# A gated mix of linear attention and a state-space convolution: masked kv left in PSUM, VectorE's work reordered in the passage between the two halves, two q products moved, and tiles placed at multiples of 256 bytes

## The chip, the cores and the metric

The kernel runs on one core of one Trainium2 chip. The metric is device time in microseconds (us), the median of the runs shown. Five engines appear: PE (TensorE; PEld is its weight load), DVE (VectorE), ACT (ScalarE), POOL (GpSimd) and SP (SyncE, which issues all DMAs).

## The reference

`x` has 2048 rows of 448. The result is a gated sum of two branches over the same `x`:

```python
g = _sigmoid((x * gate_w).sum(-1, keepdims=True))
a = _A_ref(x, A_wqkv, A_wo)              # linear attention, 16 heads of 28
b = _B_ref(x, ...) # causal convolution with a generated kernel K, plus u * D_skip
return g * a + (1 - g) * b

# in _A_ref, with phi(t) = where(t > 0, t + 1, exp(t)) + 1e-6
kv = jnp.einsum("bhsd,bhse->bhde", pk, v)
z = jnp.einsum("bhsd->bhd", pk)
num = jnp.einsum("bhqd,bhde->bhqe", pq, kv)
den = jnp.einsum("bhqd,bhd->bhq", pq, z)[..., None] + 1e-6
o = num / den                             # then @ wo
```

`kv` and `z` are sums over all 2048 rows, so no row's attention can be finished before every row's k has been read.

## The kernel before

The 2048 rows are 16 blocks of 128, numbered `c` = 0 to 15. Everything is float32; a large operand is split into a high and a low part (`split_t`, `split_n`, `k_high`, `k_low` and so on), and a product is made of high by high, low by high and high by low.

**First half.** For each block PE makes the k product of block `c + 1` (11 matmuls, tile `k` or `v1`), one or two products with a triangular matrix (tile `v`, for the convolution), the q product of block `c` (11 matmuls, tile `q`), and `do_g(c)`, which adds the block's 11 matmuls of phi(k) against x into four PSUM banks `g0` to `g3`, open over all blocks. ACT and DVE apply phi, POOL makes low parts and the skip term.

**Passage.** Block 15 is the last to go into `g`. Then, written out by hand:
`gs` is the copy of `g0..g3` to SBUF (four ACT copies). `inter` makes `z`, the carry of the convolution, and returns `carry`, one DVE instruction on the part of it that goes to `rc`. `kv_products(r)` multiplies `gs` by `wv`: for `r` = 1 heads' groups 2 and 3 into PSUM bank `k`, for `r` = 0 groups 0 and 1 into `tr`. `kv_split` multiplies the result by a block-diagonal mask (DVE, from PSUM into the SBUF tile `kv`), `kv_high` rounds it to `kvh` (ACT), `kv_low` makes `kvl`, the rest (DVE). `m_products(j)` multiplies group `j` by `wo` (three matmuls, tile `m`); `m_high` (ACT) and `m_low` (DVE) split that into the two halves of `wk2` (named `wk` in the profile) for `j` = 0 to 2 and into `shl` for `j` = 3. Four small DMAs then carry rows of `shl` into `wk2`.

**Normalization.** Per block: `norm_a(c)` is POOL's product `prod` of phi(q) by z; `norm_b(c)` is DVE's sum of it by heads (tile `den`, L530); `norm_d` is three small DVE instructions on it (L534, reciprocal L536, copy L539), below called a *den set* together with the DVE part of `norm_c`; `norm_c(c)` is one small DVE and two POOL products that give `pn`. `norm_bd` is `norm_b` and `norm_d`.

**Second half.** For each block, `turn(c)`: four PE transposes of `pn` into bank `tr`, split into `th` by ACT (high, L594) and DVE (low, L595); `tail(c)`, an ACT copy; `attend(c)`, 11 matmuls of `th` against `wk2` and `rc` (tile `a`); `final_b`, the DVE instruction that adds the two branches (tile `ot`), and its store. Loop step `c` prepares `turn(c + 1)`, `norm_c(c + 2)` and the later blocks' sums.

Within an engine instructions run in the order in which the program issues them. PSUM has eight banks: `q`, `k`, `v0`, `v1` for the whole kernel, and four that hold `g0..g3` first and two `tr` and two `a` afterwards. SBUF tiles come from pools laid out one behind the other: `const` first, then `xp`, `xt`, `xn` and `tp`. `QW` is the row pitch of the split weights `wqh` and `wql`, in float32 elements.

Of the kernel before, what the change touches and what calls it, by code (L numbers as in the profile page):

```python
# [15 lines left out]
P = 128  # L16
S = 2048
D = 448
H = 16
# [3 lines left out]
J = 4  # L23
DJ = D // J
# [5 lines left out]
PARTS = ((("x", 0), ("w", 1)), (("w", 2), ("w", 3)), (("w", 0), ("x", 1)))  # L30
FIRST = 2 * NAT + J * D
QA = 1
QW = D + 16
VS = {c: (2 * c - 10, 2 * c - 9) for c in range(5, 11)} | {c: (c + 1,) for c in range(11, NC - 1)}
SMALL = 2.0 ** -70
FLAT = 2.0 ** 35
# [1 line left out]
DS = 12  # L38
DT = 4 * (DH - DS)
# [94 lines left out]
def gated_mix_kernel(ctx: ExitStack, tc: tile.TileContext, xin, wq_d, wvo_d, abc_d, ldt_d, dsk_d,  # L134
                     turn_d, cst_d, first_d, gin_d, lag_d, out):
    nc = tc.nc
    PE, ACT, DVE, POOL, SP = nc.tensor, nc.scalar, nc.vector, nc.gpsimd, nc.sync
# [23 lines left out]
    mask, gcat, sel = cst[:DJ, :DJ], cst[:UZ, DJ:DJ + RX], cst[:, DJ + RX:]  # L161
# [15 lines left out]
    tp = work.enter_context(tc.tile_pool(name="tp", bufs=2))  # L177
# [21 lines left out]
    o = 0  # L199
    for part in PARTS:  # L200
# [8 lines left out]
        o = e  # L209
# [17 lines left out]
    def low(eng, o, r, h):  # L227
        eng.tensor_tensor(out=o, in0=r, in1=h.bitcast(F32), op=ALU.subtract)  # L228
# [78 lines left out]
    def pieces(c, wh, wl, n, tag, last=None):  # L307
        o = ps.tile([P, 512], F32, name=tag, tag=tag)
        h, l = ([xt[c][:, i + k * P:i + (k + 1) * P] for k in range(J)] for i in (0, NAT))
        hh, lh, hl = ([(a[k], w[:, k]) for k in range(J)] for a, w in ((h, wh), (l, wh), (h, wl)))  # L310
        hl = hl[1:]
        if last == "x":
            seq = hh + hl + lh
        else:
            seq = [p for k in range(J) for p in (hh[k], lh[k])] + hl
            if last == "w":
                seq = seq[2:6] + seq[8:9] + seq[6:8] + seq[9:] + seq[:2]

        def run(count):
            for _ in range(min(count, len(seq))):  # L320
                a, b = seq.pop(0)
                run.n += 1
                PE.matmul(o[:, :n], lhsT=a, rhs=b, start=run.n == 1, stop=not seq)  # L323
        run.n = 0
        return o, run
# [93 lines left out]
    w = xt[0] = xt_p.tile([P, 2 * NAT], F32R, name="xt", tag="t")  # L419
# [32 lines left out]
    qo = project(0, wqh, wql, D + 2, "q", "w")  # L452
# [3 lines left out]
    qo = project(1, wqh, wql, D + 2, "v0")  # L456
# [5 lines left out]
    for c in range(2, NC - 2):  # L462
# [17 lines left out]
        qo = project(c, wqh, wql, D + 2, "q")  # L480
# [29 lines left out]
        for j in {11: (0, 1), 12: (2, 3)}.get(c, ()):  # L510
            w = xn_p.tile([P, NX], F32R, name="wo", tag="n")[:DJ, :2 * D].rearrange("p (i d) -> p i d", i=2)
# [9 lines left out]
    pn, th, tl, pd, dn, dp = {}, {}, {}, {}, {}, []  # L521

    def norm_a(c):
        pd[c] = tp.tile([P, D], F32, name="prod", tag="pk")
        POOL.tensor_tensor(out=pd[c], in0=pq[:, c], in1=zb, op=ALU.mult)  # L525

    def norm_b(c):
        if not dp:
            dp.append(ps.tile([P, 512], F32, name="den", tag="v1")[:, :NC * H].rearrange("p (c h) -> p c h", c=NC))
        DVE.tensor_reduce(out=dp[0][:, c], in_=pd.pop(c).rearrange("p (h d) -> p h d", h=H), op=ALU.add, axis=AX.X)  # L530

    def norm_d(c, n, copy=DVE.tensor_copy):
        r = dp[0][:, c:c + n]
        DVE.scalar_tensor_tensor(out=r, in0=r, scalar=1e-6, in1=e1[:, c:c + n, None].to_broadcast([P, n, H]),  # L534
                                 op0=ALU.add, op1=ALU.mult)
# [3 lines left out]
        copy(dn[c // 2][:, c % 2:c % 2 + n], r)  # L539

    def norm_bd(c):
        norm_b(c)
        norm_d(c, 1)
# [24 lines left out]
    def gates_a(a, b):  # L568
        return og[:, a:b]
# [20 lines left out]
    def turn_split(c, o):  # L590
        t = xt_p.tile([P, 2, J, P], F32R, name="th", tag="t")
        h, l = th[c], tl[c] = t[:, 0], t[:, 1]
        ov = o.rearrange("p (j t) -> p j t", j=J)
        ACT.copy(h, ov)  # L594
        DVE.tensor_tensor(out=l, in0=ov, in1=h.bitcast(F32), op=ALU.subtract)  # L595
# [29 lines left out]
    c = NC - 2  # L625
# [7 lines left out]
    low(POOL, uw[UL:], u[UL:], uw[UL:])  # L633
    k_high(c + 1)
    k_low(c + 1)
    zh, zl = (tp.tile([P, D], F32R, name=n, tag=t) for n, t in (("zh", "w"), ("zl", "pk")))
    qo = project(c, wqh, wql, D + 2, "q")
    do_g(c, (0, 1, 2))
    zo = ps.tile([P, 512], F32, name="zo", tag="v0")
# [15 lines left out]
    for i in range(4):  # L655
        do_g(c + 1, (i,))
        ACT.copy(gs[i], g[i][:, :D])
        if i == 2:
            gates_b(gates_a(1, NC - 1), g[0])
    gates_c(NC - 2, g[0], "pkl")()  # L660
    norm_b(1)
    qo, q_run = pieces(c + 1, wqh, wql, D + 2, "q")
    for i in range(5):
        phi(i)
    gps.close()
# [41 lines left out]
        return kvp  # L707

    def kv_split(r, kvp):
        m = 3 if r else 2  # L710
        DVE.tensor_tensor(out=kv[:, 2 * r:m],
                          in0=kvp[:DJ, 2 * r * DJ:m * DJ].rearrange("p (j d) -> p j d", d=DJ),
                          in1=mask[:, None, :].to_broadcast([DJ, m - 2 * r, DJ]), op=ALU.mult)
        if r:
            a, b = (w.rearrange("p (h d) -> p h d", h=4) for w in (kvp[:DJ, 3 * DJ:4 * DJ], mask))
            DVE.tensor_tensor(out=kv[:, 3, :DT].rearrange("p (h d) -> p h d", h=4), in0=a[:, :, DS:], in1=b[:, :, DS:],
                              op=ALU.mult)
            a, b = (w[:, :, :DS].rearrange("p h (j d) -> p h j d", j=3) for w in (a, b))
            DVE.tensor_tensor(out=kv[:, 3, DT:].rearrange("p (j h d) -> p h j d", j=3, h=4), in0=a, in1=b, op=ALU.mult)

    def kv_high(r):
        rs = slice(2 * r, 2 * r + 2)
        ACT.copy(kvh[:, rs], kv[:, rs])

    def kv_low(r):
        rs = slice(2 * r, 2 * r + 2)
# [12 lines left out]
    o3 = m_products(3, ps, "k")  # L739
    o2 = m_products(2, ps, "v0")  # L740
    m_high(3, o3)
    kv_high(0)
    m_low(3, o3)
    kv_low(0)
    m_high(2, o2)
    for j in (2, 0, 1):
        SP.dma_start(out=wk2[DJ:, :, j].bitcast(F32), in_=shl[DT + 16 * j:DT + 16 * j + 16].bitcast(F32))
# [166 lines left out]
```

## Time and profile before

| | |
|---|---|
| median of 3 runs | 179.42 us (178.81, 179.42, 181.05) |
| the profiled execution | 178.89 us, of which the span from its first to its last instruction is 177.1 us |
| granted PE clock | 1.0 in all slices |
| DMA | 18.61 MB, mean 105 GB/s |

A profile row of the timeline gives the start in us from the span's start, the duration in us, the engine, the line, the operation, output <- inputs, shapes, the count, and in brackets how long the engine had been idle before and who ended the wait. Starts of neighbouring rows may overlap, since an engine begins an instruction before the one ahead has fully ended. In the chain of waits a row is start, duration and what the end of the run was waiting for at that time.

### The profile page before, as it was taken

How to read it: one execution, taken by the hardware profiler on the slowest of the kernel's cores; microseconds unless marked ns; L12 is line 12 of the kernel's file. 1: busy time of each engine (PE TensorE's matmuls, PEld its weight loads, DVE VectorE, ACT ScalarE, POOL GpSimd, SP SyncE). 2: the span in 40 equal slices, each digit the busy share in tenths (PEclk: the TensorE clock that was granted, in tenths of full speed). 3: DMA queues.
4: the chain of work that ended last, by engine and by line, in shares of the span. 5: the costliest groups of instructions: out<-in, count | busy, mean ns of one | idle time of the engine just before them, and what ended most of it. 6: DMA issues, size and time to landing. Idle time of an engine off the chain costs nothing.

```text
span 177.1 us, 2803 instructions
## 1 busy us (share of the span) xinstructions
PE 170.5 (96%) x876; PEld 151.6 (86%) x876; DVE 113.4 (64%) x244; ACT 96.2 (54%) x220; POOL 121.1 (68%) x128
## 2 busy tenths in 40 slices
PE   6999999999999999999999999999889999999991
PEld 2699999999999999999989999988678999999991
DVE  1747538698857274462824619376999988977451
ACT  3789388874536244272435753464645555564541
POOL 5167476977349969688599999439089999893100
PEclk9999999999999999999999999999999999999999
DMA  5999973095003303032133000000121212222313
GB/s 174 414 316 269 249 223 127 8 418 227 4 1 120 106 16 119 5 120 75 45 121 123 0 0 1 0 2 5 21 47 52 105 74 86 104 75 82 111 55 104
DMA packets 7963, 18.61 MB, mean 105 GB/s; under 512 B 2045, under 2 KB 4810, under 8 KB 7818
## 3 DMA queue, kind: packets, MB, share of 16 engines
q1 hardware_dynamic: 7946, 18.41, 31.6%
q8 instruction: 7, 0.11, 0.3%
q14 instruction: 10, 0.08, 0.2%
HBM read 14.38 MB, written 3.67 MB: 102 GB/s over the span
## 4 chain that ended last, share of the span: by engine, by line
PE 91%; DVE 4%; DMA 2%; ACT 1%; issue 0%; DVEq 0%; ACTq 0%
PE a L612 21%; PE g L392 20%; PE q L323 18%; PE k L323 16%; PE v L323 6%; PE tr L587 3%; DMA y<-in 2%; PE v L400 2%; PE v L399 2%; PE k L706 1%; DVE kvl L228 1%; DVE wk L694 1%; PE m L686 0%; DVE rc L677 0%; PE q L250 0%; DVE den L530 0%
## 5 line engine op out<-in xcount | busy, mean ns | idle before, releaser
L612 PE MATMUL a<-wk,th 128*128 128x448 f32 (+1 forms) x170 | 36.9, 363 | 0.7 <-DVE wk L694 0.7
L392 PE MATMUL g<-pkh,xn 128*128 128x448 f32 x112 | 35.6, 366 | 0.0
L612 PEld LDWEIGHTS a<-wk,th 128*128 128x128 f32 x170 | 29.5, 189 | 2.9 <-DVE wk L694 0.9
L323 PE MATMUL k<-wk,xt 128*128 128x448 f32 x132 | 29.6, 368 | 0.2 <-ACT wk L421 0.2
L351 DVE SCALAR_TENSOR_TENSOR k<-k,e 128x448 f32<-128x448 f32 x12 | 7.6, 632 | 32.1 <-ACT e L350 32.1
L323 PE MATMUL q<-wqh,xt 128*128 128x450 f32 x120 | 28.0, 370 | 0.0
L323 PEld LDWEIGHTS k<-wk,xt 128*128 128x128 f32 x132 | 24.6, 188 | 3.1 <-ACT wk L421 0.7
L412 POOL TENSOR_TENSOR y<-y,t 128x448 f32<-128x448 f32 x16 | 18.8, 1175 | 12.3 <-DVE t L404 11.9
L228 POOL TENSOR_TENSOR xn<-xr,xn 128x448 fp32r<-128x448 f32 x16 | 19.3, 1203 | 9.2 <-ACT xn L238 9.0
L323 PEld LDWEIGHTS q<-wqh,xt 128*128 128x128 f32 x120 | 22.5, 189 | 2.2 <-issue 0.2
L392 PE MATMUL g<-pkl,xn 128*128 128x448 f32 x64 | 23.4, 366 | 0.0
L392 PEld LDWEIGHTS g<-pkh,xn 128*128 128x128 f32 x112 | 21.0, 188 | 2.5
L349 ACT ACTIVATE e<-k 128x448 f32<-128x448 f32 x12 | 6.5, 546 | 28.0 <-PE k L323 27.9
L525 POOL TENSOR_TENSOR prod<-pq,zb 128x448 f32<-128x448 f32 x16 | 18.4, 1159 | 4.3 <-ACT zb L647 3.1
L244 POOL TENSOR_TENSOR y<-xr,rows 128x448 f32<-128x448 f32 x16 | 18.9, 1184 | 0.0
L228 POOL TENSOR_TENSOR xt<-xr,xt 128x512 fp32r<-128x512 f32 x14 | 18.2, 1299 | 0.4 <-ACT xt L232 0.4
L550 POOL TENSOR_TENSOR pn<-pq,den 128x336 f32<-128x336 f32 x16 | 12.1, 754 | 8.3 <-DVE den L539 4.4
L617 DVE SCALAR_TENSOR_TENSOR ot<-y,og,a 128x448 f32<-128x448 f32 (+1 forms) x17 | 10.6, 626 | 5.6 <-PE a L612 5.5
L595 DVE TENSOR_TENSOR th<-tr,th 128x512 fp32r<-128x512 f32 x16 | 11.0, 690 | 3.0 <-ACT th L594 2.5
L594 ACT CAST th<-tr 128x512 fp32r<-128x512 f32 x16 | 9.4, 590 | 5.5 <-PE tr L587 5.3
L392 PEld LDWEIGHTS g<-pkl,xn 128*128 128x128 f32 x64 | 11.2, 175 | 1.0
L323 PE MATMUL q<-wql,xt 128*128 128x450 f32 x45 | 11.7, 364 | 0.0
(149 smaller groups left out, 301.6 us busy)
## 6 DMA issues: line engine op xcount, KB each, us to landing
xr<-in SPq DMA_DIRECT2D x15, 512.0 KB, 6.0
out<-ot SPq DMA_DIRECT2D x15, 224.0 KB, 2.0
pq<-in SPq DMA_DIRECT2D x4, 448.0 KB
wvo<-in SPq DMA_DIRECT2D x1, 1792.0 KB
y<-in SPq DMA_DIRECT2D x2, 480.0 KB
y<-in SPq DMA_DIRECT2D x2, 450.0 KB
u<-t SPq DMA_DIRECT2D x30, 1.8 KB, 1.8
y<-in SPq DMA_DIRECT2D x1, 448.0 KB, 4.4
```

What stands on the lines that cost most here:

```text
L228: eng.tensor_tensor(out=o, in0=r, in1=h.bitcast(F32), op=ALU.subtract)
L244: POOL.tensor_tensor(out=y[:, c], in0=plain[c][:, :D], in1=dsk, op=ALU.mult)
L323: PE.matmul(o[:, :n], lhsT=a, rhs=b, start=run.n == 1, stop=not seq)
L351: DVE.scalar_tensor_tensor(out=pks[c], in0=pks[c], scalar=1.0, in1=e, op0=ALU.add, op1=ALU.max)
L392: PE.matmul(g[i][:a.shape[1], :D], lhsT=a, rhs=b, start=c == 0 and n == 0, stop=c == NC - 1 and n == len(seq) - 1)
L412: POOL.tensor_tensor(out=y[:, c], in0=y[:, c], in1=t, op=ALU.add)
L525: POOL.tensor_tensor(out=pd[c], in0=pq[:, c], in1=zb, op=ALU.mult)
L550: POOL.tensor_tensor(out=n[:, :3, :DJ].rearrange("p j (h d) -> p j h d", h=4), in0=a, in1=r[:, :H - 4].rearrange("p (j h) -> p j h", j=3)[ ...
L594: ACT.copy(h, ov)
L595: DVE.tensor_tensor(out=l, in0=ov, in1=h.bitcast(F32), op=ALU.subtract)
L612: PE.matmul(a[:, lo:hi], lhsT=u_, rhs=w_[:, lo:hi], start=n == 0, stop=n == 10)
L617: DVE.scalar_tensor_tensor(out=ot[:, lo:hi], in0=y[:, c, lo:hi], scalar=og[:, c:c + 1], in1=a[:, lo:hi], op0=ALU.mult, op1=ALU.add)
```

## The change

Five things change.

1. `kv_split` writes the masked product into the unused half of the PSUM bank that it reads, and `kv_high` and `kv_low` read it there. The SBUF tile `kv` is gone.
2. DVE's order in the passage: block 1's den set stands ahead of the kv work instead of behind `turn_split(0)`; `kv_split(0)` comes ahead of `carry`; block 2's sum and den set come behind `m_low(0)` and `m_low(1)` instead of ahead. On POOL `norm_c(1)`, `norm_a(4)` and `norm_c(2)` move with it: what stood as `prod` 2 and 3, `pn` 1, `pn` 2, `prod` 4 and 5 stands as `prod` 2, `pn` 1, `prod` 3 and 4, `pn` 2, `prod` 5. `prod` has three buffers instead of two.
3. The first two q products of block 15 stand between the blocks `g1` and `g2` of `do_g(15)` instead of behind the `z` product.
4. `QW` is 512 instead of 464, so that the rows of `wqh` and `wql` lie 2048 bytes apart instead of 1856. In the built program their four row starts, which lay 64, 128, 192 and 0 bytes past a multiple of 256, all lie 64 past one.
5. A 64-byte tile `edge` ends the pool `const`, and the `den` tile is twice as wide. The pools `xp`, `xt`, `xn` and `tp` then begin at a multiple of 256 bytes where they began 192 past one; `wk2`, `wvo`, `tri` and `both` stay 64 past one.

```diff
-QW = D + 16
+QW = 512
+EDGE = 16
...
-    kv = const.tile([DJ, J, DJ], F32, name="kv")
...
+    const.tile([P, EDGE], F32, name="edge")
...
-        pd[c] = tp.tile([P, D], F32, name="prod", tag="pk")
+        pd[c] = tp.tile([P, D], F32, name="prod", tag="pk", bufs=3)
...
-            dn[c // 2] = tp.tile([P, 2, H], F32, name="den", tag="den", bufs=3)
+            dn[c // 2] = tp.tile([P, 4, H], F32, name="den", tag="den", bufs=3)
...
         ACT.copy(gs[i], g[i][:, :D])
+        if i == 1:
+            qo, q_run = pieces(c + 1, wqh, wql, D + 2, "q")
+            q_run(2)
...
-    norm_b(1)
-    qo, q_run = pieces(c + 1, wqh, wql, D + 2, "q")
+    norm_bd(1)
+    norm_c(1)
...
     def kv_split(r, kvp):
-        m = 3 if r else 2
-        DVE.tensor_tensor(out=kv[:, 2 * r:m],
+        o = kvp[:DJ, (1 - r) * 2 * DJ:(2 - r) * 2 * DJ].rearrange("p (j d) -> p j d", d=DJ)
+        m = 2 - r
+        DVE.tensor_tensor(out=o[:, :m], ...
...
-    def kv_high(r):
-        ACT.copy(kvh[:, rs], kv[:, rs])
-    def kv_low(r):
-        low(DVE, kvl[:, rs], kv[:, rs], kvh[:, rs])
+    def kv_high(r, o):
+        ACT.copy(kvh[:, 2 * r:2 * r + 2], o)
+    def kv_low(r, o):
+        DVE.tensor_tensor(out=kvl[:, 2 * r:2 * r + 2], in0=o, in1=kvh[:, 2 * r:2 * r + 2].bitcast(F32), op=ALU.subtract)

     carry = inter()
-    q_run(2)
...
-    kv_split(1, k1)
-    kv_high(1)
+    k1 = kv_split(1, k1)
+    kv_high(1, k1)
     norm_a(3)
-    kv_low(1)
+    kv_low(1, k1)
+    k0 = kv_split(0, k0)
     carry()
-    kv_split(0, k0)
...
     q_run(2)
+    norm_a(4)
     turn_split(0, o0)
-    norm_d(1, 1)
-    norm_c(1)
-    norm_bd(2)
-    norm_c(2)
-    norm_a(4)
...
     ACT.copy(rc[0][:DT], shl[:DT, 0].bitcast(F32))
+    norm_bd(2)
+    norm_c(2)
+    norm_a(5)
     norm_bd(3)
-    norm_a(5)
```

Lines of the changed program are two to six higher. On DVE, in the first part of the passage, the order before is (`k` and `tr` are the PSUM banks of the two kv products, `m` those of the products with `wo`, which `shl` and `wk` take the low part of):

```order
L530 TENSOR_REDUCE den<-prod 128x16
L711 TENSOR_TENSOR kv<-k,cst 112x112
L716 TENSOR_TENSOR kv<-k,cst 112x64
L719 TENSOR_TENSOR kv<-k,cst 112x4x3x4
L228 TENSOR_TENSOR kvl<-kv,kvh 112x224
L677 SCALAR_TENSOR_TENSOR rc<-zs,cst,z 48x448
L711 TENSOR_TENSOR kv<-tr,cst 112x224
L694 TENSOR_TENSOR shl<-m_1354,shl 112x448
```

and now, on the same engine at the same place:

```order
L532 TENSOR_REDUCE den<-prod 128x16
L536 SCALAR_TENSOR_TENSOR den<-den,e_60 128x16
L538 RECIPROCAL den<-den 128x16
L541 COPY den<-den 128x16
L555 TENSOR_TENSOR pn<-pq,den 128x4x3x4
L718 TENSOR_TENSOR k<-k,cst 112x112
L722 TENSOR_TENSOR k<-k,cst 112x64
L725 TENSOR_TENSOR k<-k,cst 112x4x3x4
L732 TENSOR_TENSOR kvl<-k,kvh 112x224
L718 TENSOR_TENSOR tr<-tr,cst 112x224
L683 SCALAR_TENSOR_TENSOR rc<-zs,cst,z 48x448
L700 TENSOR_TENSOR shl<-m_1361,shl 112x448
```

Block 1's den set has moved ahead of the first mask, the masked products go to the PSUM tiles `k` and `tr`, and the mask for `tr` has passed the carry `rc`.

On DVE, from the split of the first transposed block to the last low part of `wk2`, the order before is:

```order
L595 TENSOR_TENSOR th<-tr,th 128x512
L534 SCALAR_TENSOR_TENSOR den<-den,e_60 128x16
L536 RECIPROCAL den<-den 128x16
L539 COPY den<-den 128x16
L553 TENSOR_TENSOR pn<-pq,den 128x4x3x4
L530 TENSOR_REDUCE den<-prod 128x16
L534 SCALAR_TENSOR_TENSOR den<-den,e_60 128x16
L536 RECIPROCAL den<-den 128x16
L539 COPY den<-den 128x16
L553 TENSOR_TENSOR pn<-pq,den 128x4x3x4
L694 TENSOR_TENSOR wk_69<-m_1400,wk_69 112x448
L694 TENSOR_TENSOR wk_69<-m_1404,wk_69 112x448
```

and now:

```order
L597 TENSOR_TENSOR th<-tr,th 128x512
L700 TENSOR_TENSOR wk_69<-m_1391,wk_69 112x448
L700 TENSOR_TENSOR wk_69<-m_1395,wk_69 112x448
L532 TENSOR_REDUCE den<-prod 128x16
L536 SCALAR_TENSOR_TENSOR den<-den,e_60 128x16
L538 RECIPROCAL den<-den 128x16
L541 COPY den<-den 128x16
L555 TENSOR_TENSOR pn<-pq,den 128x4x3x4
```

The two low parts of `wk2` come directly behind `th`; block 2's sum and den set follow them.

On PE, at the end of `do_g(15)`, the order before is:

```order
L392 MATMUL g_142<-pkl,xn 128x448
L392 MATMUL g_142<-pkh,xn 128x448
L392 MATMUL g_143<-pkh,xn 128x448
L392 MATMUL g_143<-pkl,xn 128x448
L392 MATMUL g_143<-pkh,xn 128x448
L572 MATMUL g_141<-both,og 14x128
L392 MATMUL g_144<-pkl,xn 64x448
L392 MATMUL g_144<-pkh,xn 128x448
L675 MATMUL z<-uw,gcr 112x448
L323 MATMUL q<-wqh,xt 128x450 x2
```

and now:

```order
L394 MATMUL g_142<-pkl,xn 128x448
L394 MATMUL g_142<-pkh,xn 128x448
L325 MATMUL q<-wqh,xt 128x450 x2
L394 MATMUL g_143<-pkh,xn 128x448
L394 MATMUL g_143<-pkl,xn 128x448
L394 MATMUL g_143<-pkh,xn 128x448
L574 MATMUL g_141<-both,og 14x128
L394 MATMUL g_144<-pkl,xn 64x448
L394 MATMUL g_144<-pkh,xn 128x448
L681 MATMUL z<-uw,gcr 112x448
```

The two q products stand behind the second of the four `g` banks (`g_142`), and the last two banks and `z` come behind them.

More of the change, by code (lines that the diff above doesn't have):

```diff
@@ L635, in gated_mix_kernel @@
     k_low(c + 1)
-    zh, zl = (tp.tile([P, D], F32R, name=n, tag=t) for n, t in (("zh", "w"), ("zl", "pk")))
+    zh = tp.tile([P, D], F32R, name="zh", tag="w")
+    zl = tp.tile([P, D], F32R, name="zl", tag="pk", bufs=3)
     qo = project(c, wqh, wql, D + 2, "q")
@@ L709, in kv_split @@
     def kv_split(r, kvp):
[L710 to L713 removed]
+        o = kvp[:DJ, (1 - r) * 2 * DJ:(2 - r) * 2 * DJ].rearrange("p (j d) -> p j d", d=DJ)
+        m = 2 - r
+        DVE.tensor_tensor(out=o[:, :m], in0=kvp[:DJ, 2 * r * DJ:(2 * r + m) * DJ].rearrange("p (j d) -> p j d", d=DJ),
+                          in1=mask[:, None, :].to_broadcast([DJ, m, DJ]), op=ALU.mult)
         if r:
             a, b = (w.rearrange("p (h d) -> p h d", h=4) for w in (kvp[:DJ, 3 * DJ:4 * DJ], mask))
[L716 removed]
+            DVE.tensor_tensor(out=o[:, 1, :DT].rearrange("p (h d) -> p h d", h=4), in0=a[:, :, DS:], in1=b[:, :, DS:],
                               op=ALU.mult)
             a, b = (w[:, :, :DS].rearrange("p h (j d) -> p h j d", j=3) for w in (a, b))
[L719 to L727 removed]
+            DVE.tensor_tensor(out=o[:, 1, DT:].rearrange("p (j h d) -> p h j d", j=3, h=4), in0=a, in1=b, op=ALU.mult)
+        return o
+    def kv_high(r, o):
+        ACT.copy(kvh[:, 2 * r:2 * r + 2], o)
+    def kv_low(r, o):
+        DVE.tensor_tensor(out=kvl[:, 2 * r:2 * r + 2], in0=o, in1=kvh[:, 2 * r:2 * r + 2].bitcast(F32), op=ALU.subtract)
     carry = inter()
[L730 removed]
     k1 = kv_products(1)
     k0 = kv_products(0)
[L733 to L734 removed]
+    k1 = kv_split(1, k1)
+    kv_high(1, k1)
     norm_a(3)
[L736 removed]
+    kv_low(1, k1)
+    k0 = kv_split(0, k0)
     carry()
[L738 removed]
     o3 = m_products(3, ps, "k")
@@ L741, in gated_mix_kernel @@
     m_high(3, o3)
-    kv_high(0)
+    kv_high(0, k0)
     m_low(3, o3)
-    kv_low(0)
+    kv_low(0, k0)
     m_high(2, o2)
```

## The prediction

> **What bounds the kernel now.** I read the page's busy line and its chain by engine first.
>
> ```profile
> PE 170.5 (96%) x876; PEld 151.6 (86%) x876; DVE 113.4 (64%) x244; ACT 96.2 (54%) x220; POOL 121.1 (68%) x128
> PE 91%; DVE 4%; DMA 2%; ACT 1%; issue 0%; DVEq 0%; ACTq 0%
> ```
>
> PE sets the time; only 9% of the chain is anything else. The windows by stage (us, then busy us and count for PE, PEld, DVE, ACT, POOL) say where PE is not the bound.
>
> ```profile
> 13.00:119.50 106.50, 106.50 (x526) 96.84 (x524) 64.22 (x127) 59.53 (x137) 79.53 (x70) 1.00 0.31 100
> 119.50:130.70 11.20, 9.96 (x66) 8.18 (x65) 9.26 (x28) 6.67 (x15) 6.13 (x9) 1.00 0.15 29
> 130.70:138.70 8.00, 8.00 (x43) 7.12 (x44) 7.61 (x18) 3.12 (x8) 7.83 (x11) 1.00 0.12 45
> ```
>
> In the first half PE never pauses. In the passage it does, and there and for 8 us afterwards DVE is nearly full: 9.26 of 11.2, then 7.61 of 8. The timeline of PE shows the pauses.
>
> ```profile
> 123.47 0.65 PE L686 MATMUL m<-wo,kvh 112*112 112x448 f32 x2
> 124.39 0.45 PE L686 MATMUL m<-wo,kvl 112*112 112x448 f32 x1 [0.28 <-DVE kvl L228]
> 125.11 0.66 PE L686 MATMUL m<-wo,kvh 112*112 112x448 f32 x2 [0.27 <-DVE rc L677]
> 129.33 0.66 PE L587 MATMUL tr<-both,pn 128*128 128x128 f32 x4
> 130.69 2.31 PE L612 MATMUL a<-wk,th 128*128 128x448 f32 x10 [0.70 <-DVE wk L694]
> ```
>
> A matmul of 448 columns takes about 0.203 us of PE when it is followed at once (11 in 2.24 us, quoted below), the rest of its 0.36 us is pipeline. So PE lost about 0.5 us before 124.39, 0.5 before 125.11 and, after four transposes of 0.11, 0.9 before 130.69: 1.9 us. That is all this change can win by order. DVE's timeline shows why.
>
> ```profile
> 120.50 0.27 DVE L578 TENSOR_TENSOR phs<-g,phs 14x128 fp32r<-14x128 f32 x1
> 122.17 0.27 DVE L711 TENSOR_TENSOR kv<-k,cst 112x112 f32<-112x112 f32 x1 [0.85 <-PE k L706]
> 123.13 1.21 DVE L228 TENSOR_TENSOR kvl<-kv,kvh 112x224 fp32r<-112x224 f32 x1 [0.44 <-ACT kvh L723]
> 124.37 0.69 DVE L677 SCALAR_TENSOR_TENSOR rc<-zs,cst,z 48x448 fp32r<-48x448 f32 x1
> 125.09 0.39 DVE L711 TENSOR_TENSOR kv<-tr,cst 112x224 f32<-112x224 f32 x1
> 125.99 0.38 DVE L228 TENSOR_TENSOR kvl<-kv,kvh 112x224 fp32r<-112x224 f32 x1
> 126.58 0.62 DVE L694 TENSOR_TENSOR wk<-m,wk 112x448 fp32r<-112x448 f32 x1 [0.20 <-ACT wk L690]
> 127.13 0.69 DVE L595 TENSOR_TENSOR th<-tr,th 128x512 fp32r<-128x512 f32 x1
> 127.74 0.17 DVE L534 SCALAR_TENSOR_TENSOR den<-den,e 128x16 f32<-128x16 f32 x1
> 128.63 0.63 DVE L530 TENSOR_REDUCE den<-prod 128x16 f32<-128x448 f32 x1
> 130.02 1.15 DVE L694 TENSOR_TENSOR wk<-m,wk 112x448 fp32r<-112x448 f32 x2
> 131.08 0.62 DVE L530 TENSOR_REDUCE den<-prod 128x16 f32<-128x448 f32 x1
> 135.66 0.69 DVE L595 TENSOR_TENSOR th<-tr,th 128x512 fp32r<-128x512 f32 x1
> ```
>
> The first `kvl` takes 1.21 us, the second, of the same shape, 0.38. PE's `a` waits for the low part of `wk` at 130.02, which stands behind two den sets and a sum. A den set runs from L534 to the instruction behind the set: block 1's from 127.74 to the sum at 128.63, block 2's from that sum's end, 129.26, to the low part at 130.02, about 0.8 us each.
>
> **The change part by part.**
>
> *The q products.* Two of 0.205 us (quoted under the last part) pass `g2`, `g3` and `z`, which come 0.41 us later; the kv products behind them start as before. ACT's rows show what that delays.
>
> ```profile
> 117.92 2.21 ACT L657 COPY gs<-g 128x448 f32<-128x448 f32 x4
> 120.03 0.36 ACT L577 CAST phs<-g 14x256 fp32r<-14x256 f32 x1
> ```
>
> The fourth `gs` copy, done at 120.1, will be done about 120.7. The kv products begin at 120.4 and need it for the first time six short matmuls later, about 121.0: no wait, 0.3 us in hand. `phs` behind it on ACT ends at 121.05, so DVE's `phs` starts at 121.07 instead of 120.50 and the sum of block 1 at about 121.3. The step buys nothing by itself. SP's four issues behind `phs` move by the same 0.55 us and are needed blocks later.
>
> *Block 1's den set ahead of the masks.* Sum 121.3 to 121.9, den set to 122.7, so the first mask starts about 122.65 instead of 122.17: 0.48 us late. The three masks take 0.5 as before (122.17 to 122.69, where `kvl`'s idle time of 0.44 begins; now to 123.2), ACT's `kvh` the 0.44 (123.6).
>
> *Masked kv in PSUM.* `kvl` now takes one input from PSUM. POOL's rows tell why the old one was long.
>
> ```profile
> 122.95 1.14 POOL L525 TENSOR_TENSOR prod<-pq,zb 128x448 f32<-128x448 f32 x1
> 128.50 0.75 POOL L550 TENSOR_TENSOR pn<-pq,den 128x336 f32<-128x336 f32 x1 [4.40 <-DVE den L539]
> 131.20 2.27 POOL L525 TENSOR_TENSOR prod<-pq,zb 128x448 f32<-128x448 f32 x2
> 135.47 0.40 POOL L556 TENSOR_TENSOR pn<-pq,den 128x128 f32<-128x128 f32 x1
> ```
>
> The stalled `kvl` was issued at 123.13 while `prod` ran until 124.09, and ended 0.25 us after it; the free one met an idle POOL. DVE's `th` of 0.69 us, with an input in PSUM, takes 0.69 at 135.66 too, where POOL is full. So I take 0.39, the duration of the mask at 125.09, which reads PSUM; the bounds are 0.38 and 1.21. The Trainium skill, "SBUF — State Buffer", section "Who interferes with whom", says that a VectorE instruction with two SBUF inputs contends with a GpSimd instruction that reads SBUF, and that one with at most one does not; by it the stall goes, and the two `kvl` rows agree. A price against the change is in "Perfetto Trace Analysis", section "Optimizing Scalar/DVE Operations": some 60 ns of access overhead for VectorE on SBUF and 125 on PSUM. By it the two `kvl` cost an estimated 0.13 us more in all, and the sum below would be -0.5 instead of -0.6; the rows show 0.39 against 0.38 for that shape, and I go by them.
>
> `kvl` thus ends at 124.0 instead of 124.34: the late start costs 0.48, the lost stall gives 0.82. But bank `k` now holds the masked product until `kvl` has read it, so the first two `m` matmuls, which ran at 123.47, wait too: three from 124.05, done at 124.65, as before (124.6). The mask for `tr`, 0.39, now precedes `rc`, 0.69: `rc` ends at 124.95 instead of 125.06. The next `m` matmuls start 0.1 us earlier, and the chain through `shl`, the second `kvl` and the low part at 126.58 gains 0 to 0.2 us. I take nothing up to there.
>
> *The den sets behind the low parts.* After `th` ends at 127.7 DVE goes on to the low parts. PE makes `m0` after the transposes and two q products, about 126.5 to 127.1; ACT rounds it to 127.8; so the low part runs 127.8 to 128.45, the second to 129.05, with 0.15 us of DVE idle. PE's last seven q products and four transposes end at 129.55 and `a` starts there: 1.1 us earlier than 130.69. The rows of `wk` that come by DMA could bind next.
>
> ```profile
> 126.10 2.14 SPq L747 DMA_DIRECT2D wk<-shl  x3
> 128.29 0.59 SPq L748 DMA_DIRECT2D wk<-shl  x1
> wk<-shl SPq DMA_DIRECT2D x3, 56.0 KB, 2.3
> ```
>
> The three are issued 0.7 us apart and land 2.3 us after issue: 128.4, 129.1, 129.9; the fourth 130.6. `a` needs them at its matmuls 0, 3, 6 and 9, so at 129.55, 130.2, 130.8 and 131.4. Each is in time by 0.8 us or more.
>
> *What is late next.* DVE still has block 2's sum and den set to do: 129.05 plus 0.63 plus 0.8 is 130.45, where it starts the sum that stood at 131.08. From there DVE's list is the same as before and has no idle time up to the `th` low part at 135.66. It runs 0.63 us ahead, one den set (0.8) less the 0.15 idle. PE, 1.1 us ahead, runs into it:
>
> ```profile
> 130.69 2.52 PE a L612 x11
> 136.33 2.38 PE a L612 x11
> 139.16 2.24 PE a L612 x11
> ```
>
> Before, the second row, the third `a` of the chain of waits, already took 2.38 instead of 2.24, because its second matmul waited for that low part. It will again: the part ends at 135.7 instead of 136.35, and the transposes before it wait about 0.5 us for `pn` of block 3, from DVE and from POOL. POOL does `pn` 2, two `prod`, `pn` 3 in 4.6 us from the den set's copy: 130.3 plus 4.6 is 134.9 against 135.87. So both let PE pass 0.6 us earlier, and the other 0.5 us is given back. Behind that PE is the bound again (2.24 for the fourth `a`, the last row).
>
> *Tiles at 256 bytes.* No row of before has these tiles at another place, but the q product is a comparison: in the built program its weights' row starts lie 64, 128, 192 and 0 bytes past a multiple of 256, two matmuls each. The starts of the 1st, 3rd, 5th, 7th and 9th matmul are
>
> ```profile
> 60.37 0.37 PE L323 MATMUL q<-wqh,xt 128*128 128x450 f32 x1
> 60.78 0.37 PE L323 MATMUL q<-wqh,xt 128*128 128x450 f32 x1
> 61.19 0.37 PE L323 MATMUL q<-wqh,xt 128*128 128x450 f32 x1
> 61.60 0.37 PE L323 MATMUL q<-wqh,xt 128*128 128x450 f32 x1
> 62.02 0.36 PE L323 MATMUL q<-wql,xt 128*128 128x450 f32 x1
> ```
>
> 0.41, 0.41, 0.41 and 0.42 us: the one at a multiple of 256 is no faster. I take 0. The rows resolve 0.01 us in two matmuls, so 2.5 ns each; over some 800 matmuls whose tiles move, the bounds are 2.0 us either way. The rows don't test the weight load, whose tiles all lay 192 past.
>
> **The sum.** 0 (q products, kv chain) minus 0.8 (den set out of the way) plus 0.15 (DVE's wait for `m0`) plus 0 (places) is about -0.6 us. The span goes from 177.1 to 176.5, and with the 1.8 us around it the profiled 178.89 becomes 178.3. That execution lies 0.5 under the median of 179.42; of the four executions known (178.81, 178.89, 179.42, 181.05) the middle is 179.2, and 179.2 minus 0.6 is **178.6 us**.
>
> **The rivals.**
>
> *DVE arrives late (slower).* The first mask starts 0.48 us late for certain; if `kvl` is still held, by `pn` 1 or `prod` 3, which POOL now runs there, it ends up to 0.5 us after 124.34, everything on DVE up to block 2's den set moves, and PE too. It decides from 0.6 us of lateness, where the gain above is gone; with the full 1.21 us the kv chain is 0.5 late, the mask for `tr` and ACT's roundings behind it add their own waits of up to 0.6, and the den set's copy comes at 131.4. The loss is 0.5: 179.7. Against it: `th`'s constant 0.69.
>
> *Nothing left.* PE's 1.1 us is given back wholly, because DVE's idle time grows elsewhere: 179.2. For it: DVE at 7.61 of 8 us.
>
> *No giving back.* If DVE keeps pace, the 1.1 us stays: 178.1. Against it: the same row.
>
> *The places pay.* 2.5 ns per matmul is 2.0 us, with the order 2.6: 176.6. Against it: the five q rows; for it, only that no weight load was ever seen at 0.
>
> **How the numbers follow.** The forecast has 0.5, late DVE 0.13, nothing left 0.15, no giving back 0.12, places 0.10. The range from **177.2 to 180.1** reaches past 179.7 by half of the spread of the runs and below takes in 178.1 and two thirds of the places' 2 us. The likeliest case alone is 178.1 to 179.1. Two per cent, 3.6 us, is about what a measurement of this kernel can tell from no change; no case by itself gets there, so **faster 0.04, within 0.92, slower 0.04**; the two small chances stand for places that matter more than any row shows, with either sign.
>
> **What would show it.** Right: the first `kvl` at 0.4 us; `a` starting near 129.6 with no wait for `wk`; a new wait of some 0.5 us at the transposes before the third `a`; 11 q matmuls still in 2.25 us, 11 `g` in 2.23. Wrong: `kvl` over 0.8, `a` later than 130.2, a wait for a DMA at `a`, or any matmul row that changes by over 3 ns.

## Result and profile after

The changed kernel takes 177.26 us (median of 4 runs, 177.07 to 177.85) against 179.39 for the kernel before beside it (4 runs, 178.81 to 181.05). The ratio is 0.9887, 95% interval 0.984 to 0.9934: faster by 1.1%, within the 2% that the prediction called no change, and 1.3 us under the time that it gave. The profiled execution took 177.07 us (span 175.3) against 178.89 (177.1); the granted clock is 1.0 in both. Beside e1 to e4 the kernel before took 178.6 to 179.4 us in 20 of 35 runs and 180.1 to 181.4 in 15, with none between, while no run of a kernel with the pools moved lay above 179.3; why isn't shown, and a ratio to its median holds part of that difference.

The busy line and the chain by engine of the page after, then the windows by the same three stages (their borders moved with the work; columns as in the prediction):

```profile
PE 169.2 (97%) x876; PEld 151.6 (86%) x876; DVE 114.1 (65%) x244; ACT 95.9 (55%) x220; POOL 120.5 (69%) x128
PE 85%; DVE 8%; ACT 2%; issue 2%; POOL 1%; ACTq 0%; DVEq 0%; POOLq 0%
13.00:118.50 105.50, 105.41 (x525) 96.81 (x524) 64.91 (x127) 59.01 (x136) 79.26 (x69) 1.00 0.32 101
118.50:128.70 10.20, 9.62 (x66) 8.04 (x64) 8.32 (x24) 6.03 (x14) 6.62 (x9) 1.00 0.11 22
128.70:137.40 8.70, 8.37 (x45) 7.09 (x44) 8.11 (x22) 3.88 (x10) 7.71 (x11) 1.00 0.16 54
```

PE is busy 1.3 us less although the number of its instructions (876) is the same. Matmuls themselves run closer together, and the order alone doesn't do that: it is 170.9 in e4 below, 169.6 with the places alone (e3). The first window shows it: 525 matmul rows in 105.5 us, where 526 took 106.5. The chain of waits gives the rate. First four rows of before, then the same stretch of after, each 11 matmuls (start, duration):

```profile
63.20 2.23 PE g L392 x11
65.43 2.24 PE k L323 x11
68.08 2.27 PE q L323 x11
139.16 2.24 PE a L612 x11
```

```profile
62.60 2.23 PE g L394 x11
64.83 2.21 PE k L325 x11
67.44 2.21 PE q L325 x11
140.46 2.21 PE a L614 x11
```

`q` takes 0.06 us less in this stretch, `k` and `a` 0.03, `g` nothing. The other part is the passage. PE's timeline there:

```profile
119.29 1.83 PE L712 MATMUL k<-gs,wvo 128*112 128x112 f32 x16
123.11 0.66 PE L692 MATMUL m<-wo,kvh 112*112 112x448 f32 x2 [0.42 <-DVE kvl L732]
124.14 0.66 PE L692 MATMUL m<-wo,kvh 112*112 112x448 f32 x2 [0.16 <-DVE rc L683]
128.31 0.60 PE L589 MATMUL tr<-both,pn 128*128 128x128 f32 x4
128.67 2.25 PE L614 MATMUL a<-wk,th 128*128 128x448 f32 x10
131.32 2.52 PE L614 MATMUL a<-wk,th 128*128 128x448 f32 x10
134.38 0.63 PE L589 MATMUL tr<-both,pn 128*128 128x128 f32 x4 [0.33 <-DVE pn L555]
134.76 2.41 PE L614 MATMUL a<-wk,th 128*128 128x448 f32 x10
```

The wait for `wk` at the first `a` (0.70 in the rows of before) is gone: `a` follows its transposes at once. A new wait stands at the transposes before the third `a`, and the second `a` takes 2.52 us for ten matmuls. DVE's timeline shows the kv chain and what follows the low parts:

```profile
121.41 0.28 DVE L718 TENSOR_TENSOR k<-k,cst 112x112 f32<-112x112 f32 x1
121.72 0.23 DVE L722 TENSOR_TENSOR k<-k,cst 112x64 f32<-112x64 f32 x1
121.98 0.22 DVE L725 TENSOR_TENSOR k<-k,cst 112x48 f32<-112x48 f32 x1
122.66 0.39 DVE L732 TENSOR_TENSOR kvl<-k,kvh 112x224 fp32r<-112x224 f32 x1 [0.47 <-ACT kvh L729]
123.39 0.69 DVE L683 SCALAR_TENSOR_TENSOR rc<-zs,cst,z 48x448 fp32r<-48x448 f32 x1
127.06 1.23 DVE L700 TENSOR_TENSOR wk<-m,wk 112x448 fp32r<-112x448 f32 x2 [0.24 <-ACT wk L696]
128.20 0.62 DVE L532 TENSOR_REDUCE den<-prod 128x16 f32<-128x448 f32 x1
131.63 1.35 DVE L532 TENSOR_REDUCE den<-prod 128x16 f32<-128x448 f32 x2
```

So that runs can be compared stage by stage, the table below gives the time between five fixed PE starts of each profiled execution: the first `k` product, the first kv product, the first `a`, the transposes before the fourth `a`, and the last matmul. The changes of order lie in the two in the middle.

| kernel | k to kv | kv to `a` | `a` to transposes | to the end | time of the runs, ratio to before |
|---|---|---|---|---|---|
| before | 115.18 | 10.29 | 7.87 | 34.62 | 179.39 |
| after | 114.25 | 9.38 | 8.55 | 34.21 | 177.26, 0.9887 |
| places only (e3) | 114.60 | 10.28 | 7.85 | 34.25 | 177.75, 0.9891 |
| order only (e4) | 115.22 | 9.42 | 8.56 | 34.61 | 178.76, 0.998 |
| q products back (e8) | 114.36 | 9.06 | 8.54 | 34.22 | 176.95, 0.9852 |
| masked kv in SBUF (e9) | 114.22 | 9.27 | 8.54 | 34.22 | 177.15, 0.9842 |
| block 1's den set late (e10) | 114.22 | 9.25 | 8.77 | 34.25 | 177.23, 0.9847 |
| three edits (e11) | 114.32 | 9.05 | 7.87 | 34.31 | 176.68, 0.9817 |

After minus before is -0.93, -0.91, +0.68, -0.41. The order gains 0.91 and gives 0.68 back; the places give the rest, 1.34, and 0.17 more lies before the first `k`, where kernels with the same start-up differ by as much (4.89 us in e8, 5.20 in e9).

### The profile page after: what moved, and what is told of

The parts are those of the page before. It is cut to its first block, busy times and chain, and to the rows that moved or that the text cites. A ratio compares the mean times of both kernels' runs of the same rounds, so it can differ in the third digit from the quotient of the medians.

```text
span 175.3 us, 2809 instructions
## 1 busy us (share of the span) xinstructions
PE 169.2 (97%) x876; PEld 151.6 (86%) x876; DVE 114.1 (65%) x244; ACT 95.9 (55%) x220; POOL 120.5 (69%) x128
## 4 chain that ended last, share of the span: by engine, by line
PE 85%; DVE 8%; ACT 2%; issue 2%; POOL 1%; ACTq 0%; DVEq 0%; POOLq 0%
PE g L394 19%; PE a L614 18%; PE q L325 17%; PE k L325 14%; PE v L325 6%; PE tr L589 4%; PE q L252 2%; PE v L402 2%; DVE den L532 2%; PE v L401 2%; PE m L692 1%; DVE wk L700 1%; DVE den L538 1%; POOL xn L230 1%; ACT gs L660 1%
## 5 line engine op out<-in xcount | busy, mean ns | idle before, releaser
L325 PE MATMUL q<-wqh,xt 128*128 128x450 f32 x120 | 27.4, 365 | 0.0
```

## Experiments

### Which part pays: places or order

**e1**: before, with only the pitch of `wqh` and `wql` changed.

```diff
-QW = D + 16
+QW = 512
```

> The kernel before with only the row pitch of wqh and wql changed from 1856 to 2048 bytes; pools still begin 192 past a multiple of 256. Theory pitch (the q weights' unequal starts cost, nothing else does): 11 q matmuls fall from 2.265 to 2.21 us, k stays 2.235, the time falls by about 0.9 us. Theory distance (what counts is how far the two operands' starts lie apart modulo 256): all four q starts now have k's distance of before, so q takes k's 2.235 and the time falls by 0.5. Theory stationary (what counts is that the loaded weights' tile begins at a multiple of 256): no row changes, 0.

179.21 us, ratio 0.9993 (0.9959 to 1.0026). In its chain of waits the intervals are those of before (2.25 to 2.27 for `q`, 2.23 or 2.24 for `k`):

```profile
62.59 2.26 PE q L323 x11
67.48 2.23 PE k L323 x11
```

All q rows now start 64 past a multiple of 256, and that alone is worth nothing. (In the first half of the profiled execution, 180.91 us, PE waits 1.06 us for DVE's `pq`, a wait that the profile of before doesn't have.)

**e2**: before, with only 64 bytes at the end of the pool `const`, so that the tiles loaded as weights (`xt`, `th`) start at a multiple of 256 instead of 192 past one.

```diff
+    const.tile([P, 16], F32, name="edge")
```

> The kernel before with only a 64-byte tile behind the constants, so that the pools xp, xt, xn and tp begin at a multiple of 256; the pitch of wqh and wql stays 1856. Theory pitch: k and a fall from 2.235 to 2.21 at most, q stays 2.265, the time falls by 0.6. Theory stationary: q falls to 2.21 and k and a to 2.21, -1.4 us. Theory distance: k and a fall to 2.21, q, whose four starts keep four different distances, stays near 2.265: -0.6.

178.28 us, ratio 0.995 (0.9914 to 0.9987).

```profile
64.89 2.21 PE k L324 x11
67.51 2.26 PE q L324 x11
```

`k` is as fast as in the changed kernel, `q` as slow as before. Neither e1 nor e2 helps `q` alone.

**e3**: before, with everything that moves a tile (pitch, 64 bytes, the `den` tile's width) and no change of order.

```diff
-QW = D + 16
+QW = 512
...
+    const.tile([P, 16], F32, name="edge")
...
-            dn[c // 2] = tp.tile([P, 2, H], F32, name="den", tag="den", bufs=3)
+            dn[c // 2] = tp.tile([P, 4, H], F32, name="den", tag="den", bufs=3)
```

> The kernel before with all of the placing (pitch, 64-byte tile, wider den tile) and none of the order or of the masked kv in PSUM. If the placing brings what the changed kernel's rows say (q 2.21, k and a 2.21, g as before), the time falls by 1.4 to 1.6 us of the 2.1 that the whole change brings, and the passage keeps its pauses of 0.5, 0.5 and 0.9 us. The prediction's reading, that places cost nothing, expects 0.

177.75 us, ratio 0.9891 (0.9857 to 0.9925): by the ratio as much as the whole change, by the median 0.5 us less. Its profile shows 0.98 us less than before in the stages, and its passage has the pauses of before (row "places only").

**e4**: the changed kernel without the places.

```diff
-QW = 512
-EDGE = 16
+QW = D + 16
...
-    const.tile([P, EDGE], F32, name="edge")
...
-            dn[c // 2] = tp.tile([P, 4, H], F32, name="den", tag="den", bufs=3)
+            dn[c // 2] = tp.tile([P, 2, H], F32, name="den", tag="den", bufs=3)
```

> The changed kernel with the placing undone (pitch 1856, no 64-byte tile, narrow den tile): order and masked kv in PSUM alone. The prediction's sum expects -0.6 us against the kernel before, with the first kvl at 0.39, a starting 1.1 us earlier in the passage and 0.5 us given back at the transposes before the third a. From the changed kernel's rows I expect -0.3 to -0.4. If the placing were without effect it would show the whole -2.1.

178.76 us, ratio 0.998 (0.9937 to 1.0023). The runs can't tell this from nothing; the stages of its profile say -0.88 and +0.69, so about -0.2. Both the gain and what is given back stand in it as in the changed kernel: neither has to do with the places.

### What about the places

**e5**: the changed kernel with the moving rows and the pools all at a multiple of 256.

```diff
-EDGE = 16
+EDGE = 32
...
+    const.tile([P, 48], F32, name="head")
```

> The changed kernel with 192 bytes more in front of wk2 and 64 more behind the constants, so that wk2, wqh and wql begin at a multiple of 256 as the pools do; order unchanged. Theory multiple (a matmul is fast when its tiles begin at a multiple of 256): q and k stay at 0.200 to 0.201 us per matmul or get faster, 2.21 us or less per 11. Theory distance (fast when the moving operand begins 64 bytes further than the loaded weights, modulo 256): q and k lose it, k goes to 2.235 and q to 2.25 per 11, like g, which has distance 0; the time rises by about 1.2 us.

```profile
65.33 2.23 PE k L326 x11
67.96 2.23 PE q L326 x11
```

178.31 us in one run. `k` is as slow as before, `q`, at 2.23 to 2.25, loses more than half of its gain: a start at a multiple of 256 is not what pays.

**e6**: the changed kernel with everything 64 bytes farther (moving rows at 128, pools at 64).

```diff
+    const.tile([P, 16], F32, name="head")
```

> The changed kernel with 64 bytes more in front of wk2, so that every tile behind it moves by 64: weights' rows 128 past a multiple of 256, pools 64 past one, distances as in the changed kernel. Theory multiple: nothing begins at a multiple of 256, q goes to 2.25 or more and k to 2.235 per 11, the time rises by 1.2 us. Theory distance: 2.21 for both, no change.

```profile
60.71 2.21 PE q L326 x11
65.55 2.21 PE k L326 x11
```

As fast as the changed kernel, at other places: what stays the same is the distance of 64 bytes from the start of the tile loaded as weights to the start of the moving one. The one run took 177.84 us, with a wait of 0.51 us for DVE's `wk` among the first products.

**e7**: the changed kernel with 64 bytes between the pools `xn` and `tp`, so that `g` too has that distance (`pkh`, `pkl` at 64, `xn` at 0); it was 0 before and after.

```diff
+    gap = work.enter_context(tc.tile_pool(name="gap", bufs=1))
+    gap.tile([P, 16], F32, name="gap")
```

> The changed kernel with a 64-byte tile between the pools xn and tp, so that pkh and pkl, the moving operands of g, begin 64 past a multiple of 256 while the loaded x stays at 0: the distance of the fast q and k matmuls. Theory distance: 11 g matmuls fall from 2.23 to 2.21 us, 16 blocks, -0.3 us; q, k and a stay. Theory multiple: g loses a tile at a multiple of 256 and gets slower or stays, 0 to +0.5 us.

```profile
63.25 2.21 PE g L396 x11
```

`g`, which the change had left at 2.23, gets the same 2.21. The total is 177.61 us (0.9871, 0.9794 to 0.9947), no better than the changed kernel. Its 16 blocks of `g` should save 0.3 us; in its profile the first products take longer (seven `k` matmuls 2.19 us, 1.68 in the changed kernel), and PE waits 0.26 us for POOL's `xn`.

**e12**: the changed kernel with the pools 128 bytes farther, which puts `k`, `q` and `a` at distance 192.

```diff
-EDGE = 16
+EDGE = 48
```

> The changed kernel with the pools 128 bytes farther: the moving rows of wk and wq still start 64 past a multiple of 256, the tiles loaded as weights (xt, th) now at 128, so that the moving operand starts 192 past the loaded one instead of 64; g stays at distance 0. Theory (only the distance of 64 is fast): 11 k, 11 q and 11 a take 2.235 to 2.245 us, 203 to 205 ns a matmul, about 1.2 us in all over some 520 matmuls, and the total is that of the change of order alone, near 178.4. Rival (any distance that is 64 off a multiple of 128 is fast): 200 to 201 ns, 2.21 us, and the total that of the changed kernel, near 177.3.

```profile
65.83 2.22 PE k L325 x11
68.45 2.27 PE q L325 x11
```

178.65 us, ratio 0.9961 (0.9934 to 0.9989): the gain of the places is gone, and what is left is near the order alone (e4). `q` loses its gain as the theory said, by more than expected, and is slower than at 0; `k` at 2.22 is nearly as fast as at 64, against the 2.235 to 2.245 expected. Distance alone doesn't give all intervals. The chains of waits give together, in us for 11 matmuls (448 columns; 450 for `q`):

| distance of the moving start from the loaded one, modulo 256 | k | q | a | g |
|---|---|---|---|---|
| 0 | 2.23 (e5) | 2.23 to 2.25 (e5) | 2.22 to 2.24 (e5) | 2.22 to 2.23 (before, after) |
| 64 | 2.20 to 2.22 (after, e2, e6) | 2.20 to 2.22 (after, e6) | 2.21 to 2.22 (after, e6) | 2.20 to 2.22 (e7) |
| 128 | 2.23 to 2.24 (before) | 2.24 to 2.27 (e1) | 2.24 to 2.25 (before) | |
| 192 | 2.22 (e12) | 2.26 to 2.27 (e12) | 2.22 to 2.24 (e12) | |
| all four, in turn | | 2.25 to 2.27 (before), 2.26 to 2.27 (e2) | | |

The table holds for most products and not for all. In after and e6 three of the 14 `q` products counted take 2.27 us at the distance of 64, those that directly follow a `k` product with no `v` product between (2.25 in before); two do in e7 and e11 (2.26 and 2.27), and three in e5 at 0. So the place alone doesn't settle the interval: what runs ahead of a product counts too. How is not known. No distance that isn't a multiple of 64 was tried.

### What the order does

**e8**: the changed kernel with the two q products behind `z` again.

```diff
-        if i == 1:
-            qo, q_run = pieces(c + 1, wqh, wql, D + 2, "q")
-            q_run(2)
...
+    qo, q_run = pieces(c + 1, wqh, wql, D + 2, "q")
...
+    q_run(2)
     k1 = kv_products(1)
```

> The changed kernel with the two q products behind z again. The prediction's reading (the step buys nothing by itself) expects the time within 0.1 us. Rival: since the copies of g, phs and so block 1's sum on DVE come 0.4 us earlier again, the first mask starts 0.2 to 0.35 us earlier and the kv chain with it; a starts 0.2 to 0.3 us earlier against the end of g, of which the loop's start gives some back: -0.2 us.

176.95 us (176.71 to 177.19), ratio 0.9852 (0.9778 to 0.9926); kv to `a` 9.06 instead of 9.38, the other stages within 0.11. Its PE and DVE rows:

```profile
119.25 1.73 PE L710 MATMUL k<-gs,wvo 128*112 128x112 f32 x16
121.02 0.28 DVE L716 TENSOR_TENSOR k<-k,cst 112x112 f32<-112x112 f32 x1
```

The first mask starts 1.77 us after the first kv product, as before the change (120.39 to 122.17), where it takes 2.12 in the changed kernel (119.29 to 121.41). So block 1's den set costs the first mask nothing as long as the q products keep their old place. The moved q products alone cost it little too (e10 below: 1.86 us); only both together make it late.

**e9**: the changed kernel with the masked kv in SBUF again.

```diff
+    kv = const.tile([DJ, J, DJ], F32, name="kv")
...
-        o = kvp[:DJ, (1 - r) * 2 * DJ:(2 - r) * 2 * DJ].rearrange("p (j d) -> p j d", d=DJ)
+        o = kv[:, 2 * r:2 * r + 2]
```

> The changed kernel with the masked kv written to its SBUF tile again, all else as changed. Theory (the PSUM place is what makes the first kvl short, because POOL's pn 1 is at work beside it): kvl is issued near 122.66, ends only when POOL's pn does, near 123.05 to 123.4, so it takes 0.6 to 0.8 us instead of 0.39; but the bank of k comes free when the masks end, so the first two m matmuls start near 122.6 instead of 123.1 and PE loses less in that one pause. Total 0 to 0.4 us slower than the changed kernel. Rival (it was the order of POOL's work, not the place, that made kvl short): kvl 0.38 here too, and the total 0 to 0.3 us faster than the changed kernel since the bank is free earlier.

177.15 us (176.96 to 177.57), ratio 0.9842 (0.978 to 0.9905); kv to `a` 9.27. DVE, then POOL and PE beside it:

```profile
121.53 0.27 DVE L719 TENSOR_TENSOR kv<-k,cst 112x112 f32<-112x112 f32 x1
121.72 0.21 DVE L723 TENSOR_TENSOR kv<-k,cst 112x64 f32<-112x64 f32 x1
121.85 0.20 DVE L726 TENSOR_TENSOR kv<-k,cst 112x48 f32<-112x48 f32 x1
122.49 0.58 DVE L733 TENSOR_TENSOR kvl<-kv,kvh 112x224 fp32r<-112x224 f32 x1 [0.44 <-ACT kvh L730]
124.73 1.05 DVE L733 TENSOR_TENSOR kvl<-kv,kvh 112x224 fp32r<-112x224 f32 x1
122.07 0.75 POOL L553 TENSOR_TENSOR pn<-pq,den 128x336 f32<-128x336 f32 x1
123.29 2.24 POOL L528 TENSOR_TENSOR prod<-pq,zb 128x448 f32<-128x448 f32 x2
122.59 0.64 PE L693 MATMUL m<-wo,kvh 112*112 112x448 f32 x2
```

Both `kvl` are longer while POOL works (0.58 and 1.05 against 0.39 and 0.38), so the mechanism of the change is real. It gains nothing: the three masks take 0.52 us from the first start to the last end when they write SBUF (121.53 to 122.05) and 0.79 when they write PSUM (121.41 to 122.20), and the first `m` matmuls, whose bank is free earlier, start at 122.59 instead of 123.11. The 0.27 us are waits: in the built program of the changed kernel the second and the third mask each wait for the mask before, which writes the tile `k` that they read; in before and in e9, where the masks write `kv`, they wait for no other mask.

**e10**: the changed kernel with block 1's den set behind `turn_split(0)` again; block 2's stays behind the low parts.

```diff
-    norm_bd(1)
-    norm_c(1)
+    norm_b(1)
...
-    norm_a(4)
     turn_split(0, o0)
+    norm_d(1, 1)
+    norm_c(1)
+    norm_a(4)
```

> The changed kernel with block 1's den set back behind the split of block 0's transposes, where it stood before; block 2's set stays behind the low parts. Theory (the time is bound by how early DVE and POOL come to pn of block 3; the early set of block 1 is what buys this): the first mask starts about 0.4 us earlier and a 0.1 us earlier or later, but the wait at the transposes before the third a grows from 0.7 to 1.2 or more; total 0.4 to 0.8 us slower than the changed kernel. Rival (the set of block 1 ahead of the masks costs what it gains): total within 0.2 us of the changed kernel.

177.23 us (177.17 to 177.5), ratio 0.9847 (0.9785 to 0.9909); kv to `a` 9.25, `a` to transposes 8.77. The rival is right: 0.13 won, 0.22 given back. PE waits longer inside the second `a` (0.67 us from its first matmul to its second, 0.45 in the changed kernel). The last two rows give the first mask, 1.86 us after the first kv product:

```profile
131.86 2.08 PE L614 MATMUL a<-wk,th 128*128 128x448 f32 x9 [0.23 <-DVE th L597]
134.47 0.63 PE L589 MATMUL tr<-both,pn 128*128 128x128 f32 x4 [0.33 <-DVE pn L555]
119.30 1.82 PE L711 MATMUL k<-gs,wvo 128*112 128x112 f32 x16
121.16 0.28 DVE L717 TENSOR_TENSOR k<-k,cst 112x112 f32<-112x112 f32 x1 [0.51 <-PE k L711]
```

**e11**: three edits that the runs point to: the q products as in e8, the 64 bytes of e7, and block 2's sum in DVE's idle time behind `carry`, where DVE waits for ACT's rounding of group 3's product (from the end of `rc`, 124.08, to 124.58 in the changed kernel).

```diff
     carry()
+    norm_b(2)
...
-    norm_bd(2)
+    norm_d(2, 1)
```

> The changed kernel with three edits: the two q products behind z and the kv products' masks again as before, a 64-byte tile that puts pkh and pkl at 64 past a multiple of 256 and leaves xn at 0, and block 2's sum moved up to the place where DVE waits for m3. Theory (places: distance 64; give-back: DVE's list up to pn of block 3): g 11 in 2.21 instead of 2.23, worth 0.3 us; the q products' return 0.3; the wait before the third a falls from 0.7 to 0.2 or less, worth 0.5; total 1.0 us under the changed kernel, so near 176.2, ratio 0.983. Rival (what is given back is given back elsewhere, and places of g cost a wait at the start): total 0.2 to 0.4 under the changed kernel, near 176.9, ratio 0.986.

176.68 us (176.34 to 177.04), ratio 0.9817 (0.9769 to 0.9864): the lowest median of all, between what the theory and the rival expected; its runs overlap with those of e8 (176.71 to 177.19). `a` to transposes is 7.87 again, with kv to `a` at 9.05: next to nothing is given back. The other two edits don't do it, for that stage is 8.54 in e8 and 8.55 in e7. PE's rows:

```profile
89.89 0.47 PE L404 MATMUL v<-xn,tri 128*128 128x448 f32 x1 [0.29 <-POOL xn L232]
131.09 2.25 PE L616 MATMUL a<-wk,th 128*128 128x448 f32 x10
133.47 0.63 PE L591 MATMUL tr<-both,pn 128*128 128x128 f32 x4
```

The second `a` takes 2.25 instead of 2.52, and the transposes start 0.1 us after its last matmul is issued. The 0.3 us of `g` don't arrive: k to kv is 114.32 against 114.36 in e8, and the first row shows a new wait for POOL, of 0.29 us. PE, further ahead of POOL here, waits for it.

## Why the prediction was right or wrong

**The time**: 178.6 was forecast for the median, 177.26 measured; 1.3 us too much, under the likeliest case's own 178.1 to 179.1. The class, within 2%, was right. That the time still lies inside the range (177.2 to 180.1), by 0.06 us, is luck: the lower end took in two thirds of the places' bound, a case with a chance of 0.10. Nearly all of the miss is one term.

**Tiles at 256 bytes: the step that failed.** It was put at 0 with bounds of 2.0 us either way, and measured about -1.3 by the stages (e3 alone: ratio 0.9891). The step read the q rows, in which moving starts of 64, 128, 192 and 0 follow each other, found 0.41 us for each pair, and concluded that a place doesn't matter. Four things were wrong in that. The test varied the start of the moving tile and asked whether it is a multiple of 256, where what counts most is its distance from the tile loaded as weights (e5, e6). The rows did hold the good distance once in four, the start of 0 against loaded weights at 192, and it was no faster there; a mixed sequence was no test of an even one. (In the median of the trace's 14 `q` products that pair takes 0.416 us in before, and 0.400 at the same place in the changed kernel. In e2 the pair at 64 stands first, with 0.406 as in the changed kernel; since the first pair takes 0.408 in e5 too, at distance 0, that decides nothing.) And the step itself named what it had not tested, the weight load, and then took the middle of the bounds. And those bounds were too tight: starts that are rounded to 0.01 us tell 5 ns a matmul in a pair, not 2.5. The rival "the places pay" had the mechanism and 2.5 ns a matmul; measured are some 5 ns for `q` (0.05 to 0.06 us in 11), 2 to 3 for `k` and `a`, 0 for `g`.

The Trainium skill, "SBUF — State Buffer", section "Who interferes with whom", gives PE two read ports, one for the moving operand and one for the weight load, and calls them independent. Taken by itself it lets one expect that their places relative to each other cost nothing. The rows differ by up to 3% with that place, and the measurement decides; whether port or memory behind it makes the difference, no run here shows.

**The q products** were to buy nothing and cost nothing. They cost 0.3 us by the stages (e8). The delay of `phs` and of block 1's sum was read rightly (0.9 us after the first kv product by the prediction, 0.75 in the trace, 120.04 against 119.29), but the lateness was booked to the den set alone. With the q products in their old place the den set hides in DVE's wait for the kv product, 0.85 us idle in the rows of before (e8); with them moved and the den set late the first mask comes 1.86 us after the first kv product (e10), with both 2.12. The fourth `gs` copy is also needed sooner than the prediction said, at the fourth matmul of the first kv product and not six matmuls later: the 16 matmuls take 1.82 or 1.83 us in every profile with the q products moved, and 1.73 in the others.

**Masked kv in PSUM**: `kvl` 0.39 us, exactly as predicted, and the first mask late by 0.34 instead of 0.48. But "the three masks take 0.5 as before" was wrong: 0.79. The two errors partly cancel; `kvl` ends 3.76 us after the first kv product where it ended 3.95 after it (-0.19; predicted -0.34), and "I take nothing up to there" held: the second `m` pair starts 4.85 after instead of 4.72. The Trainium skill, "Perfetto Trace Analysis", section "Optimizing Scalar/DVE Operations", has some 65 ns more access overhead for VectorE on PSUM than on SBUF. The prediction weighed it where `kvl` reads PSUM, and there the rows show 0.01 (0.39 against 0.38). Where the masks write PSUM, their own durations grow by as little (0.28, 0.23 and 0.22 against 0.27, 0.21 and 0.20 in e9). What the masks lose is something else: their starts are 0.31 and 0.26 apart into PSUM, 0.19 and 0.13 into SBUF, because in the tile `k` each waits for the one before, as said at e9. The prediction had no such wait.

**Low parts ahead of block 2's den set**: `a` was to start 1.1 us earlier relative to the kv products, and starts 0.91 earlier, without a wait for `wk`; no transfer of `wk`'s rows became a wait, as predicted. This is what the order gains. e10, where block 1's den set is late again, has a first `a` that is earlier still (9.25).

**What is late next**: the new wait was predicted at the transposes before the third `a`, of some 0.5 us, and stands there (previous matmul issued to 133.88, transposes at 134.38). Another 0.27 is lost inside the second `a`, which waits for `th`'s low part behind DVE's longer list: its second and third matmul start 0.45 and 0.31 us after the ones ahead, where the first `a` has 0.29 and 0.20. That wait was not foreseen. So 0.77 instead of 0.5 is lost, of which 0.68 shows in the stage, since the `a` matmuls themselves are faster now. The explanation by DVE's list is shown by e11: one sum of 0.62 us taken out of it, and the stage is 7.87 again, as before. The order's sum, -0.6, was therefore too kind by 0.2 of lost time at each end: -0.2 measured (e4), which the runs can't tell from 0.

**The rivals**: "DVE arrives late" needed a held `kvl`, and it ran free at 0.39; "nothing left" is near the truth for the order alone, though it is 0.2 us off it by the stages; "no giving back" is refuted by the 0.68; "the places pay" came true at two thirds of its price. That 11 q matmuls would stay at 2.25 us was named as a sign; they take 2.21, and any matmul row that changes by over 3 ns was named as a sign of being wrong.

## What to carry to other kernels

Where PE is the bound, compare the start-to-start time of like matmuls in different tiles before any order is touched: one to three per cent of it, over some 540 matmuls of `k`, `q`, `v` and `a`, were worth several times what the new order of the passage kept (1.3 us against 0.2). To test a place, move all tiles of a stage together, the loaded and the moving one, and try the other distances; a mixed sequence says little of an even one. In a passage where one engine's list is nearly full, what counts is the idle time of that list: a moved set of instructions pays if it falls into such a place, as block 2's sum does in e11. And a tile that is written where it is read can bring new waits between instructions that had none, as the masks show.

## What the runs showed of the hardware

The interval of float32 matmuls with 448 to 450 columns depended on where their two SBUF operands start relative to each other: 2.20 to 2.22 us for 11 at a distance of 64 bytes modulo 256, 2.22 to 2.27 at 0 and 128, 2.22 to 2.27 at 192 (2.22 for `k`, 2.27 for `q`), at granted clocks of 0.997 to 1.0. That is not the whole rule, for three of 14 `q` products at 64 took 2.27. Why 64 is mostly the good one, why `k` and `q` differ at 192, and how the product ahead comes into it, stays open.

A VectorE instruction that waits for the one ahead started 0.31 us after it, 0.03 after its recorded end; without the wait the same instruction started after 0.19 us, 0.08 before that end (second mask, after and e9).
